# Softmax denominators of a four-stage attention and mixing kernel: the last 64 keys added on VectorE, two head pairs per group of ones-products

## The chip, the cores and the metric

The kernel runs on one core of one Trainium2 chip. The metric is the device time of one execution in microseconds (us), as the median of several runs.

## The reference, cut to what matters

Inputs are `q`, `k`, `v` of shape (4 batches, 12 heads, 448 positions, 64), a number `cap`, and the weights of two mixing blocks.

```python
scores = scale * q @ k.T                       # per head, 448 x 448
scores = cap * tanh(scores / cap)
attn = exp(scores - max(scores))
attn = attn / (sum(attn) + 1e-9)               # the denominators
x = attn @ v                                   # heads side by side: (4, 448, 768)

theta = x @ w_theta                            # first block, d_model 768
y = w_tok_r @ (x * cos(theta)) + w_tok_i @ (x * sin(theta))
u = x + y
x = u + relu(u @ w_ch)

h = (relu(x.T @ w_tok1) @ w_tok2).T            # second block
u = x + h
out = u + relu(u @ w_ch1) @ w_ch2              # 768 -> 1536 -> 768
```

All of it is computed in float32 accuracy. Attention multiplies in plain float32 (scores of batches 2 and 3 as three products of split numbers); the mixing blocks split each factor into a high and a low part and sum three products.

## The kernel before

**Attention.** The 12 heads of a batch are worked on as 6 pairs, and `(b, hp)` names a pair (24 in all). Scores are kept transposed: keys on the partitions, the 448 queries along the free axis. A pair has its 448 keys in three chunks of 128 (c = 1, 2, 3) and a tail of 64 (c = 0). A chunk holds both heads, `[128, 2, 448]`. The tails of an even pair and of the odd pair after it share one tile `tm`: one half of the partitions for either head, the halves swapped for the odd pair. `scores` (line 1027) does a chunk's products, then tanh and exp on ScalarE over 128x896; `av` (line 1062) multiplies exp(scores) by `v` into a PSUM tile; `LAG` chunks lie between the two.

**Denominators.** `sums` (line 1077) runs after each chunk of `av`. VectorE adds chunks 2 and 3 to chunk 1 in place (`SUMS`). At the pair's last chunk TensorE multiplies by ones: two products over the tail (with `mine`, which picks a head's half of the partitions) and two over the summed chunks, each into 32 rows of one PSUM tile, with the four side by side in the array. The tail's share and the chunks' share thus land in different rows and are added later. There is one such group per pair. For batches 2 and 3 the sums share a two-bank PSUM tile (`pa`, which the scores use too) with the pair's output; for 0 and 1 both are single banks of `pm` (`ACCM`).

**Closing a pair.** The output must be multiplied by 1/denominator, spread over the 64 rows of each head. There are two ways. `close` (line 1097, batch 0, all six pairs) stays on the engines: VectorE copies the output out of PSUM and the sums with eps/2 added; TensorE regroups the sums with four small products by `sel`; VectorE takes reciprocals and spreads them along a diagonal; TensorE multiplies by `spread`; VectorE scales the output. `finish` (line 1122, the other 18 pairs) copies output and sums out on VectorE, sends the sums by DMA into a compact tile `pk`, adds and inverts them, writes them to DRAM (`sr`) and reads them back spread over 64 rows each (`dn`, two DMAs). For batches 0 and 1 the result is then split: the high part on VectorE, the low part `XHL[..., 1]` on GpSimd. For 2 and 3 it is stored to DRAM.

**What sets the order.** All instructions are recorded first and ordered by a planner (`Plan`, line 333): a simulated schedule with a cost per instruction, a priority for each one (its place in the recording plus a shift from the packed table `RANKS`), and a limited number of buffers per tag (`SB`, `PS`). The order that comes out is written to each engine's in-order queue. The recording starts with `FIRST` steps of attention; `token(0, (0,))`, the first half of the first block for batch 0, is then woven with `SECOND` more, and what is left of the attention with batch 1 and the layers behind. Each weight piece is once fetched, split into a high and a low part and cached (`convert`, line 776); `CV` says which engine does each of its four steps (scale, low, high, rest) in each phase. `EVC` gives the engine for copies out of PSUM in `sums` and `close`, for batches 0 and 1 and for 2 and 3. `TS` and `TS0` are the buffer tags that hold the exp tiles in turn.

Of the kernel before, what the change touches and what calls it, by code (L numbers as in the profile page):

```python
# [20 lines left out]
ALU = mybir.AluOpType  # L21
# [3 lines left out]
P = 128  # L25
# [15 lines left out]
EVC = 'vv'  # L41
LAG = 3
GRP = (1, 1, 1, 1)
TS = ("t", "t", "t", "ex", "ex")
TS0 = TS
AHEAD = 2
SB = {'kq': 2, 'vt': 2, 'hl': 1, 't': 3, 'tm': 2, 'sv': 2, 'dn': 1, 'xr': 2, 'pk': 3, 'rq': 2, 'w': 4, 'raw': 3, 'cw': 5, 'wg': 4, 'zx': 5, 'rc': 4, 'ex': 2}
PS = {'pa': 2, 'pm': 4, 'ph': 4}
LATEPS = ('pm', 'ph')
SUMS = ('vv','vv')  # L50
CV = ('vaav','aaav','aaav')
# [28 lines left out]
CLOSE = 1  # L80
# [4 lines left out]
ACCM = 2  # L85
QREC = 'v'
NATIVE = 2
SVA = 0
# [3 lines left out]
FIRST = 30  # L92
SECOND = 24
# [5 lines left out]
c-mE)1$Y%#(D&zt1PuiO#R*V6#odY&mjcC#yE_z$2MDeW?(Pl&in|tf4Z(s03rUa!a(CX};oSG__whW-y?1xdoSFapN6y*J@-YLn)Xfjtv0sdy>-  # L99
140b9~bEUq0%Z+c8=$=A+&`8l$B*#AsUIkGf-ej3(+DrT*JubXj<e22_gC8be}q{N`v~(I#5&1V-  # L100
!qRUb91e~f1C_)*_H|EN`Ke%9?5Vsz@BPa5+vT5DJStY4eO>A8bnG<(|^Efe}hU4dWq=M7)=qEEDbIq*UM{VQ58-t&<()xPSR8ecWTyJ+3x#Om!6U-
cK~t4<Nsl>_4RaP2P|FvhLDt~h$IkD~*x@IBZ^&Y%6NpQ^@c*U65KAL3|XKUM#WZr$42(Lt9T-
P_R7oiT3p{p8lL#Xb^z)UD0(xV8T_AIWmq(M;JL^_>%;r)#-&;6@)=)E61CZq1)wHT_h#R^HEeA4fY3b#&BtN6SugwC{2s>7P_})=IZ#TIwUiBHUWFs-rW
0bu`^aw??&abnqW;T@~oodc_>QvCh%*{;I<U`iS2FM=z9cwA2_M88XDJY5Mv|)SWo}mQM9;LmxTb%SR%^-Fo_@TNh_QN9N1c$kEC1-
cmWzt)UAXT|LLq9eGuIquaGAjy`p%K78S5NMhAFtyNRcaP*Hdsw-y3>D-%c^}g#Z{~-
U#0=FLa_mQP{94($!wP6<3%R3w$Rz>win4?h(9lh_ZI?3he+C)BbIL@tA{!r~2>n$CgxV21IM{nj*z4g-
3d2JlsUO_c7jq1xxs?9IBwQ=&KGVYeQOm3)JA3sIz_Lf1F-1_Obw}h^DbU{<qiT`?w>xiS{z#-
zGxBS4I5f2@8cDvP|u_J1z9?Rh9q_K|XjdAq!b#Ez_$w#KagGL=4^={$TI|UuhRT~|PsOJ9Q*1KuEMK*d%o<^!Ed{zBUdds)DsufG6kY6%8dbqgi)}4+X`
p3~d<sCi3TvsMI+B$IpS-HYn4%Sr71aHpq{rSOoUGlrP_<&E66sl*JdrP%B-jeWd)n26>UAD+u!Vam1u5~o*nwJDNSM9LH(X{w|^WFp!-
dVL0K5@YPM2Mp&x4L!A=Xkw*E?!q4GcaMCR#=r>!bf;Z44C@uQ+?gRTap!of4AYVx1&YiZ17Asaq8%mS&ps<ax`wcw*+?gmK;|d9gZHuyLijP`)+MASEPu  # L110
aqj};T{RzJRRUd47Ia>NJ)q=$xeNq6NdV5RzCXR0T;^^@n-g3Mfa(jA9$Wm-vLOj*;mYU_=`XRBSr&f5$y=;zlEa|8}7+r6V4?j7YK1I9^bnfZOORDEvc}
x9rK63w*qq813S`i=TL{4h_b)**h1~X4qNB>OVEe8fWdar?_x9WOJ)s(8a-n+H#JM23I7q`208yNd0Qf=oWvM65l@JH2-
i@c;A_to#H+WMiFWcG7wzJp$}<A_`56>)S^YcCns!b=M7b@Z1u@mja3mn56!)?B^ZdfVkCA;`a8NwwA<N1I-CYq4F9-
X7%EhztC#tXiR#YKZ`1CCbt6W59d<1<g}9UWfR4$v+d_dal2tUHf`TmJF&*q1Gw%>W6;S6NqTE>fZMX=~dT9D7JaY3+{VWO|^D$FR7J{_}iumeYJ>7zW*B
?t2*E<`Y>!1GA4gjjV^}H`1XmHqf6sl(x(qO<d{oJw<F(GSM9siC3DDW?TF)QeO*FG>g~O%M&7R(y(BEDqrDS4+O6|5Z8TPO<_4EsIik8PsYuvo)htn}G0
fEvU00_N`T9(?96JB}#wC8lqWhYoKL@#F$UtzotoreqYJ!heeix74&MV^hDf%EYVw+3GlvVZWs#<2WODb%D+Xq~-2cve*Q+=P`CE>$F+Wf0}pLui-
`Q@r=*i$RB_Xd8SP;Iqb^~xJnZd1~vKHACse7_c_8g$RzI}iO2bMFLnE_p?@2l;H{EHHGeUX?>tueTLRi~O0_?3hs(RR6#?kL@i|5t+DHw<dK-
B4RZBA$BwtX&0l~{*)ba;*07!=Ed!@4_$&dm*$gdLdKQ42aab%ZYE41UG|A|-z(DdACW$LMEdO(`E!>@u9M`{52`sMRjcn1Ir-ko4cjhq1id?L;s?B$3Vx
Z$8B_4zO6FRP{^!qO1HYdigi4&NiLV}G|GUwui{4=u7#-kzTaH%Te<8WZ6z*xp?~GSPZh2WdOTfLovzdP;^IlY)3f^yasdmRd=fI-
{K3sD{)d#x@aJ?d!9%ZZ#$I0`mUB;jrI3#xCn?RA4aC#nmKkLC!mZ*~YwE19>gv&$%mx%nn3VaufoOw=-  # L120
WNaQ}y&(^s^zdi(29Z7R@25?wozXcQ{ttswsHKNrtENo|FB4kvgt$(8L`)JBA2w6FnY%k<`g2T4Br*~F3gDyN$?g5`h^?pS`Ynk_A<lhbo{Qg*kDS@)k&k
PFe<#DMiW|YRugD8*7I0aMtrIv7jusizPox9(M%5D;ItW>}$^Y>8ZK$=O2lmbzMZELfWq3)942Ey_uM_jc*?f3+WEI>Grv|=Ig=P}M{6$y8`3b5Gx`-
@KDUy@%y*lw9I=#g<x7*79?mM;LNkMuR8H32jQbr^}Y5Y@4BymZR<R##FIeY()#Km&*NZ;Q?vS8B!#&@hEvJxMU28VLbt-O}`M20_5-
# [36 lines left out]
|PXsfa5u1JbgF4$`<%<8o2Z1jc0H<SpjkoJiVQte2o0=a4jUS-  # L160
EYW@jO(m}BZ%wU;6I2pu8Z8X7mQDU+f4ix$oE9}ARkzlCdr+`?uz7=<y(-?{9EB|dOj1N!&hv-LSI)3T{9E&3ujYTP-iIl;5PAH9h<9p{Pi23^*J2;Rbel
As~bH(bLHwH@)Q0m-
P^4h@!4N}RPWuk`(Lx+NhW;P7@vgEkMw6f?Dx0bmzjnQ|ExkE@Vx~eQ)0729rVX9Ly4UN_^2B`EXo?Q#BcN)#B8ZLw%0Rtt}MM`1=gD7!Dtz|t0I2AX4cK
bc>wqqC?`?~taERN2gF;qS&SvF#<P~0#P|ZtodNt8Q1h-Fh9l&nwk96HzbpM-WpM38uIWy_t$@sq^dM!?e*}Ii#`pYiX9E3uXL8^~a&lJm{~5bF@R<vKeA
~|Y@wwf%*~yr*TpRCMhqR>@7G<1SubVxGrR2>%#7cE|(vrMTjPvcdw+y}51^oP{>CdQ*A;j6Ay+t|=XMURhf%wSHJhka@?!wtN<f@P4-E-
# [448 lines left out]
def attn_mix_kernel(ctx: ExitStack, tc: tile.TileContext, kqd, vd, cap, wu, wtok, wt1, wt2, out):  # L614
# [94 lines left out]
    consts = const("consts", [5])  # L709
    capt, qscale, eps, halfpi, eps2 = (consts[:, i:i + 1] for i in range(5))  # L710
    sel = const("sel", [32])
    spread = const("spread", [P])
# [1078 lines left out]
```

## Time and profile before

| | us |
|---|---|
| median of 3 runs (lowest to highest) | 883.93 (883.5 to 884.7) |
| profiled execution | 883.66 |
| its span | 881.9 |
| TensorE (PE) busy | 869.8 (99%) |
| VectorE (DVE) busy | 727.6 (83%) |
| ScalarE (ACT) busy | 539.3 (61%) |
| GpSimd (POOL) busy | 190.2 (22%) |

The profiled execution took 1.8 us more than its span. A busy TensorE is one with a matmul in flight: matmuls overlap, so what a group of them costs is the distance from its first start to the next group's first start, not the sum of durations. A plain float32 matmul stands in the trace as two records. TensorE's clock was granted in full in every slice of the span. Nearly all instructions go through one recording helper and so carry one line number; groups are told apart by their tiles. Batch 0's attention lies in about the first 76 us, all attention in the first 368 us.

### The profile page before, as it was taken

Reading aid. Unit: us, or ns where it says so; the run is one execution under the profiler, and the core shown is the slowest. Engines: PE = TensorE matmul, PEld = TensorE weight load, DVE = VectorE, ACT = ScalarE, POOL = GpSimd, SP = SyncE. Lnnn points to the kernel's source line nnn. Section 1 sums busy time; section 2 is a strip of 40 time slices with the busy share of each in tenths; the row PEclk is TensorE's granted clock in tenths of the full one; section 3 lists DMA queues with packets and bytes.
Section 4 is the critical chain, followed back from the end, with each engine's and each line's share of the span. In section 5 each row is a group of like instructions: output and inputs, shape, how many; then the busy total and the mean of one; then the engine's idle time right before and its main releaser. Section 6 shows DMA issues by size and latency. Waiting matters only on the chain. (4 is left out here: it accounts for less than half of the span.)

```text
span 881.9 us, 13457 instructions
## 1 busy us (share of the span) xinstructions
PE 869.8 (99%) x4683; PEld 684.8 (78%) x4683; DVE 727.6 (83%) x1363; ACT 539.3 (61%) x929; POOL 190.2 (22%) x163
## 2 busy tenths in 40 slices
PE   9989999999999999999999999999999999999998
PEld 2224665657677667699999899899999999999997
DVE  6999889997875665799898899889968778958597
ACT  7998999789974565456475563755533445334251
POOL 2434232330121110012333343132210130000000
PEclk9999999999999999999999999999999999999999
DMA  6888775684478342146888898812124112745623
GB/s 194 298 307 292 224 262 182 215 275 140 147 206 311 123 140 77 48 130 221 286 298 258 312 331 297 313 37 73 42 83 151 36 54 85 227 132 190 203 88 122
DMA packets 85320, 163.35 MB, mean 185 GB/s; under 512 B 11268, under 2 KB 65156, under 8 KB 85252
## 3 DMA queue, kind: packets, MB, share of 16 engines
q1 hardware_dynamic: 85252, 162.49, 55.9%
q8 instruction: 37, 0.61, 0.3%
q14 instruction: 31, 0.25, 0.1%
HBM read 114.75 MB, written 47.58 MB: 184 GB/s over the span
## 5 line engine op out<-in xcount | busy, mean ns | idle before, releaser
L598 POOL TENSOR_TENSOR cw<-cw,raw 128x384 uint32<-128x384 uint32 (+2 forms) x94 | 106.0, 1133 | 295.4 <-DVE cw L598 117.4
L598 PE MATMUL tm<-WT,zn 128*128 128x448 f32 x504 | 112.1, 371 | 0.0
L598 PEld LDWEIGHTS tm<-WT,zn 128*128 128x128 f32 x504 | 92.4, 188 | 16.0 <-issue 6.6
L598 PE MATMUL P<-XHL,w 128*128 128x448 f32 x414 | 91.9, 364 | 0.0
L598 PE MATMUL c<-g,w 128*128 128x448 f32 x432 | 88.3, 364 | 0.0
L598 PEld LDWEIGHTS c<-g,w 128*128 128x128 f32 x432 | 81.0, 187 | 6.4
L598 ACT ACTIVATE t<-sp,consts 128x896 f32<-128x896 f32 x72 | 71.9, 1013 | 18.9 <-PE sp L598 17.4
L598 PEld LDWEIGHTS P<-XHL,w 128*128 128x128 f32 x414 | 77.5, 188 | 6.0
L598 ACT ACTIVATE t<-t,consts 128x896 f32<-128x896 f32 x72 | 75.0, 1053 | 0.7
L598 PE MATMUL P<-T,S 128*128 128x448 f32 x306 | 68.5, 365 | 0.9 <-ACT u L598 0.9
L598 ACT CAST w<-cw 128x384 fp32r<-128x384 f32 x72 | 36.5, 517 | 51.1 <-POOL cw L598 18.3
L598 PE MATMUL av<-t,vt 128*64 128x448 f32 x288 | 64.6, 556 | 1.6 <-DVE sv L598 0.7
L598 POOL TENSOR_TENSOR XHL<-XT,XHL 128x448 fp32r<-128x448 f32 x30 | 40.0, 1333 | 119.5 <-ACT XHL L598 95.0
L598 PEld LDWEIGHTS P<-T,S 128*128 128x128 f32 x306 | 57.2, 188 | 5.7 <-ACT u L598 1.3
L598 DVE TENSOR_TENSOR t<-t,t 128x896 f32<-128x896 f32 x48 | 53.4, 1112 | 3.9 <-PE av L598 2.9
L598 DVE SCALAR_TENSOR_TENSOR cw<-raw,cw 128x384 uint32<-128x384 uint32 (+2 forms) x94 | 52.5, 565 | 1.0
L598 ACT ACTIVATE raw<-raw 128x384 uint32<-128x384 uint32 (+2 forms) x94 | 48.5, 527 | 4.6 <-DMA raw<-wu 4.5
L598 PE MATMUL sp<-kq 64*128 64x448 f32 (+1 forms) x240 | 46.9, 573 | 3.6 <-ACT t L598 3.6
L598 ACT CAST S<-F 128x256 fp32r<-128x256 f32 (+1 forms) x57 | 24.5, 445 | 41.7 <-DVE F L598 38.0
L598 PE MATMUL th<-XHL,w 128*128 128x448 f32 x216 | 49.2, 372 | 0.0
L598 DVE TENSOR_TENSOR w<-cw,w 128x384 fp32r<-128x384 f32 x72 | 42.9, 601 | 7.5 <-ACT w L598 7.5
L598 PE MATMUL P<-g,S 128*128 128x448 f32 x216 | 48.6, 368 | 0.0
(163 smaller groups left out, 1797.1 us busy)
## 6 DMA issues: line engine op xcount, KB each, us to landing
w<-cu SPq DMA_DIRECT2D x40, 768.0 KB
raw<-wu SPq DMA_DIRECT2D x72, 384.0 KB
cu<-w SPq DMA_DIRECT2D x52, 384.0 KB
kq<-kqd SPq DMA_DIRECT2D x24, 448.0 KB
cu<-w SPq DMA_DIRECT2D x10, 768.0 KB
w<-cu SPq DMA_DIRECT2D x27, 256.0 KB
cs<-S SPq DMA_DIRECT2D x30, 192.0 KB
S<-cs SPq DMA_DIRECT2D x30, 192.0 KB
```

Of the source, the lines that this page charges most:

```text
L598: getattr(eng[o.eng], name)(*map(real, a), **{x: real(y) for x, y in k.items()})
```

## The change

VectorE adds the tail's two halves to chunk 1 as well (two adds of 64 partitions x 448 per pair), so one tile per pair holds all that is to be summed. `finish` is called once per two pairs, and its group of four products by ones (two heads of two pairs, 32 rows each) serves both. Only one double pair, `(0, 4)` (the last of batch 0), closes by products, with one `sel` step and two products by `spread`; the others go by DMA, one `pk` and one `sr` transfer per two pairs. Output and sums of batches 0 and 1 are copied out of PSUM by ScalarE (`EVC`), their low part is made by VectorE (`XLO`), and the output tile is always a single bank of `pm`. For weight pieces the low step of the first 11 goes from ScalarE to VectorE; from the 12th on, the scale step goes from VectorE to ScalarE. `FIRST` grows by 3 and `SECOND` falls by 3, the tags of the exp tiles change, `rq` has one buffer instead of two, and `RANKS` is another table (left out here).

```diff
-EVC = 'vv'
+EVC = 'av'
-TS = ("t", "t", "t", "ex", "ex")
-TS0 = TS
+TS = ('ex','t','t','t','t','t')
+TS0 = ('ex','zx','zx','zx','t','zx')
-CV = ('vaav','aaav','aaav')
+CVN = 11
+CLOSE = ((0, 4),)
+TAIL = 'vv'
+XLO = 'v'
+CV = ('vvav','aaav','aaav')
-FIRST = 30
-SECOND = 24
+FIRST = 33
+SECOND = 21
...
-        scale, low, high, rest_ = CV[phase[0]]
+        scale, low, high, rest_ = CV[phase[0] or int(len(done) >= CVN)]
...
         def accs(b, hp):
-            if b < ACCM:
-                acc = [psum("av"), None]
-            else:
-                acc2 = psum2("av")
-                acc = [acc2[:, 0], acc2[:, 1]]
-            st[b, hp][3] = acc
+            st[b, hp][3] = [psum("av"), None]
...
         def sums(b, hp, c, acc, pt):
+            odd = hp % 2
+            if c >= 2:
+                (pool if SUMS[b // 2][c - 2] == "p" else dve).tensor_tensor(out=pt[1], in0=pt[1], in1=pt[c], op=ALU.add)
+            if c == odd:
+                for j in range(2):
+                    r = rows(j ^ odd)
+                    (pool if TAIL[b // 2] == "p" else dve).tensor_tensor(out=pt[1][r, j], in0=pt[1][r, j], in1=pt[0][r], op=ALU.add)
+            if c == (NM if odd else 0):
+                x = XT[:, b, hp, :] if b < 2 else sbuf("xr", "xr", [S])
+                (act.copy if EV[b // 2] == "a" else dve.tensor_copy)(x, acc[0][:, :S])
+                st[b, hp][3] = x
+                if odd:
+                    finish(b, hp - 1)
+
+        def close(b, hp, sm):
             sv = sbuf("sv", "sv", [S])
+            dve.tensor_scalar(out=sv, in0=sm[:, :S], scalar1=eps, scalar2=None, op0=ALU.add)
             rq = sbuf("rq", "rq", [CP])
             with plan.fuse():
                 for q in range(NK):
+                    mm(sm[32 * q:32 * q + 32, :CP], sel, sv[:, q * CP:(q + 1) * CP], True, True, f32=True, half=0.25)
+            dve.reciprocal(out=rq, in_=sm[:, :CP])
...
+            for n in range(2):
+                dn = sm if n else psum("dn")
+                mm(dn[:, :S], spread[:, n], sv, True, True, f32=True)
+                scaled(b, hp + n, st[b, hp + n][3], dn[:, :S])
+
+        def finish(b, hp):
+            sm = psum("sm")
+            with plan.fuse():
+                for n in range(2):
+                    for j in range(2):
+                        g = 64 * n + 32 * j
+                        mm(sm[g:g + 32, :S], ones, st[b, hp + n][4][1][:, j, :], True, True, f32=True, half=0.25)
+            if (b, hp) in CLOSE:
+                return close(b, hp, sm)
+            sv = sbuf("sv", "sv", [S])
+            (act.copy if EV[b // 2] == "a" else dve.tensor_copy)(sv, sm[:, :S])
+            pk = sbuf("pk", "pk", [2, 16])[:4 * S // 16, 0]
+            sr = dram(f"sr{b}_{hp}", 4, [S], whole=True)
+            with pri(-50):
+                sp_.dma_start(pk, sv[::32].then(lambda a: a.rearrange("q (p f) -> q p f", f=16)))
+            dve.tensor_scalar(out=pk, in0=pk, scalar1=eps[:4 * S // 16], scalar2=None, op0=ALU.add)
+            dve.reciprocal(out=pk, in_=pk)
...
+            for n in range(2):
+                x = st[b, hp + n][3]
+                dn = sbuf("dn", "dn", [S])
+                with pri(-50):
+                    for j in range(2):
+                        sp_.dma_start(dn[64 * j:64 * j + 64], sr[2 * n + j:2 * n + j + 1].then(lambda a: a.broadcast_to([64, S])))
+                scaled(b, hp + n, x, dn)
+
+        def scaled(b, hp, x, dn):
+            dve.tensor_tensor(out=x, in0=x, in1=dn, op=ALU.mult)
             if b >= 2:
                 stash[b, hp] = dram(f"xd{b}_{hp}", P, [S])
                 sp_.dma_start(stash[b, hp], x)
             else:
                 dve.tensor_copy(out=XHL[:, b, hp, 0], in_=x)
-                lo_pool(XHL[:, b, hp, 1], x, XHL[:, b, hp, 0])
+                (lo_pool if XLO == "p" else lo)(XHL[:, b, hp, 1], x, XHL[:, b, hp, 0])
             del st[b, hp]
```

## Rows read from the trace of the kernel before

**Rows 1.** The page, part 1: busy time, share, instructions of TensorE.

```profile
PE 869.8 (99%) x4683; PEld 684.8 (78%) x4683; DVE 727.6 (83%) x1363; ACT 539.3 (61%) x929; POOL 190.2 (22%) x163
```

**Rows 2.** Windows of 20 us: busy time (instructions) per engine, granted clock, DMA share, GB/s.

```profile
20.00:40.00 20.00, 18.91 (x102) 5.32 (x103) 19.12 (x33) 20.00 (x29) 9.62 (x7) 1.00 0.92 312
40.00:60.00 20.00, 18.70 (x120) 5.09 (x116) 20.00 (x38) 20.00 (x29) 7.62 (x7) 1.00 0.79 270
60.00:80.00 20.00, 18.32 (x101) 7.59 (x98) 18.28 (x38) 17.02 (x24) 9.13 (x8) 1.00 0.88 305
...
100.00:120.00 20.00, 20.00 (x111) 11.72 (x111) 18.43 (x37) 19.92 (x35) 7.23 (x7) 1.00 0.82 254
...
280.00:300.00 20.00, 20.00 (x132) 15.35 (x131) 11.02 (x19) 9.11 (x13) 3.70 (x3) 1.00 0.48 163
```

**Rows 3.** Timeline of TensorE, 158 to 176 us: start, duration, engine, operation, count.

```profile
159.86 0.57 PE L598 MATMUL sm<-tm,mine 128*32 128x448 f32 x2
...
160.75 0.98 PE L598 MATMUL tp<-ident,rc 128*128 128x128 f32 x7
```

**Rows 4.** Timeline of TensorE, 60 to 80 us, with idle before in brackets.

```profile
61.14 1.02 PE L598 MATMUL sm<-sv,spread 128*128 128x448 f32 x2
62.09 1.02 PE L598 MATMUL sp<-kq 64*128 64x448 f32 x4
64.43 1.02 PE L598 MATMUL sp<-kq 64*128 64x448 f32 x4 [1.33 <-ACT t L598]
...
68.68 0.40 PE L598 MATMUL sm<-sv,sel 128*32 128x112 f32 x8
69.01 1.77 PE L598 MATMUL sp<-kq 64*128 64x448 f32 x8
...
76.50 3.70 PE L598 MATMUL th<-XHL,w 128*128 128x448 f32 x17
```

**Rows 5.** Groups by line and shape: operation, shapes, count; busy us, mean ns; idle before.

```profile
L598 PE MATMUL sm<-t,ones 128*32 128x448 f32 x48 | 11.3, 551 | 0.0
...
L598 PE MATMUL av<-t,ones 128*32 128x448 f32 x48 | 11.2, 550 | 0.0
```

**Rows 6.** The same view: VectorE and ScalarE operations that go, move or stand nearest.

```profile
L598 ACT ACTIVATE raw<-raw 128x384 uint32<-128x384 uint32 x72 | 39.6, 560 | 4.6 <-DMA raw<-wu 4.5
...
L598 ACT COPY u<-P 128x448 f32<-128x448 f32 x34 | 18.0, 529 | 29.7 <-PE P L598 29.0 <-DVE u L598 0.7
...
L598 DVE TENSOR_TENSOR XHL<-XT,XHL 128x448 fp32r<-128x448 f32 x24 | 16.3, 692 | 2.5 <-ACT XHL L598 2.5
...
L598 DVE TENSOR_TENSOR hl<-kq,hl 128x448 fp32r<-128x448 f32 x12 | 14.9, 1244 | 0.2
...
L598 DVE COPY XT<-av 128x448 f32<-128x448 f32 x12 | 7.4, 617 | 0.5 <-PE av L598 0.5
...
L598 DVE TENSOR_SCALAR cw<-raw 128x384 f32<-128x384 f32 x12 | 5.5, 466 | 3.9 <-DMA raw<-wu 3.9
...
L598 DVE RECIPROCAL rq<-sm 128x112 f32<-128x112 f32 x6 | 5.0, 847 | 0.4 <-PE sm L598 0.2
...
L598 DVE TENSOR_SCALAR sv<-sm,consts 128x448 f32<-128x448 f32 x6 | 4.1, 680 | 0.6 <-PE sm L598 0.5
...
L598 DVE TENSOR_TENSOR sv<-rq,diag 128x448 f32<-128x448 f32 x6 | 3.7, 620 | 0.0
...
L598 ACT ACTIVATE cw<-raw 128x224 f32<-128x224 f32 x8 | 3.2, 406 | 1.2 <-DVE ch L598 1.2
```

**Rows 7.** The tile `dn`: shortest/median/longest ns, first and last start, us.

```profile
L598 DVE TENSOR_TENSOR XT<-XT,dn x6: 611/615/619, 102.3 to 185.1; 128x448 f32<-128x448 f32 x6
```

**Rows 8.** The tile `pk`, same columns.

```profile
L598 SPq DMA_DIRECT2D pk<-sv x36: 502/562/867, 78.4 to 369.6; - x36
```

**Rows 9.** Timeline of VectorE, 60 to 80 us.

```profile
67.02 0.61 DVE L598 COPY XT<-av 128x448 f32<-128x448 f32 x1
67.55 1.35 DVE L598 TENSOR_TENSOR t<-t,t 128x896 f32<-128x896 f32 x1
```

More of the change, by code (lines that the diff above doesn't have):

```diff
@@ L104 @@
[L104 to L109, printed above, removed]
@@ L256 @@
+hvL|~9!v_F{|AA61L2ATJ{>oEAY?er^BvRwn(rd1nH!k95niP?`<DaMFKjBq^*ZQ39bZ4EzdAn+ec*Zk1>pYyR_A<6
 """
@@ L708, in attn_mix_kernel @@
     ident = plan.buf(lambda: ident_ap, "con", [P])
-    consts = const("consts", [5])
-    capt, qscale, eps, halfpi, eps2 = (consts[:, i:i + 1] for i in range(5))
+    consts = const("consts", [4])
+    capt, qscale, eps, halfpi = (consts[:, i:i + 1] for i in range(4))
     sel = const("sel", [32])
-    spread = const("spread", [P])
+    spread = const("spread", [2, P])
     diag = const("diag", [NK])
-    pick = const("pick", [2])
+    pick = const("pick", [4])
     ones = const("ones", [32])
-    mine = const("mine", [2, 32])
     kq0 = sbuf("kq", "kq", [2, S])
@@ L721, in attn_mix_kernel @@
     dve.memset(ones, 1.0)
-    dve.memset(mine, 0.0)
-    for j in range(2):
-        dve.memset(mine[64 * j:64 * j + 64, j], 1.0)
     with pri(30):
@@ L727, in attn_mix_kernel @@
         dve.memset(diag, 0.0)
-        for j in range(2):
-            for g in range(2):
-                dve.memset(sel[64 * g + 32 * j:64 * g + 32 * j + 1, 16 * j:16 * j + 16], 1.0)
+        for g in range(4):
+            dve.memset(sel[32 * g:32 * g + 1, 8 * g:8 * g + 8], 1.0)
         for q in range(NK):
             dve.memset(diag[32 * q:32 * q + 32, q:q + 1], 1.0)
-        for j in range(2):
-            at = pick[:, j:j + 1]
-            cols = [ident[:, 32 * q + 16 * j:32 * q + 16 * j + 1] for q in range(NK)]
+        for g in range(4):
+            at = pick[:, g:g + 1]
+            cols = [ident[:, 32 * q + 8 * g:32 * q + 8 * g + 1] for q in range(NK)]
             dve.tensor_tensor(out=at, in0=cols[0], in1=cols[1], op=ALU.add)
@@ L738, in attn_mix_kernel @@
                 dve.tensor_tensor(out=at, in0=at, in1=cols[q], op=ALU.add)
-            dve.tensor_copy(out=spread[:, 64 * j:64 * j + 64], in_=at.then(lambda a: a.broadcast_to([P, 64])))
+            dve.tensor_copy(out=spread[:, g // 2, 64 * (g % 2):64 * (g % 2) + 64], in_=at.then(lambda a: a.broadcast_to([P, 64])))
     dve.memset(halfpi, HALFPI)
@@ L745, in attn_mix_kernel @@
     dve.tensor_scalar(out=eps, in0=eps, scalar1=1e-9, scalar2=None, op0=ALU.mult)
-    dve.tensor_scalar(out=eps2, in0=eps, scalar1=0.5, scalar2=None, op0=ALU.mult)
     wt = sbuf("warm", "zx", [S])
@@ L1077, in sums @@
         def sums(b, hp, c, acc, pt):
-            mode = SUMS[b // 2]
-            end = NM if hp % 2 else 0
-            if c >= 2 and mode[c - 2] != "n":
-                (pool if mode[c - 2] == "p" else dve).tensor_tensor(out=pt[1], in0=pt[1], in1=pt[c], op=ALU.add)
-            own = [0, 1] + [i for i in (2, 3) if mode[i - 2] == "n"]
-            todo = range(len(own)) if c == end else ()
-            if todo and acc[1] is None:
-                acc[1] = psum("sm")
-            with plan.fuse():
-                for i in todo:
-                    src = pt[own[i]]
-                    for j in range(2):
-                        g = 64 * (i % 2) + 32 * j
-                        js = slice(64 * j, 64 * j + 64)
-                        a1, a2 = (mine[:, j ^ (hp % 2)], src) if own[i] == 0 else (ones, src[:, j, :])
-                        plan.rec("PE", "matmul", (acc[1][g:g + 32, :S], a1, a2), {"start": i < 2, "stop": i >= len(own) - 2}, {"f32": True, "half": 0.5 if i == 2 else 0.25})
-            if c == end:
-                finish(b, hp, acc)
-        def close(b, hp, acc):
-            x = XT[:, b, hp, :] if b < 2 else sbuf("xr", "xr", [S])
-            (act.copy if EV[b // 2] == "a" else dve.tensor_copy)(x, acc[0][:, :S])
+            odd = hp % 2
[12 more added lines that the diff above has]
+        def close(b, hp, sm):
             sv = sbuf("sv", "sv", [S])
-            if SVA:
-                act.activation(sv, acc[1][:, :S], AF.Identity, bias=eps2)
-            else:
-                dve.tensor_scalar(out=sv, in0=acc[1][:, :S], scalar1=eps2, scalar2=None, op0=ALU.add)
+            dve.tensor_scalar(out=sv, in0=sm[:, :S], scalar1=eps, scalar2=None, op0=ALU.add)
             rq = sbuf("rq", "rq", [CP])
@@ L1107, in close @@
                 for q in range(NK):
-                    mm(acc[1][32 * q:32 * q + 32, :CP], sel[:, :32], sv[:, q * CP:(q + 1) * CP], True, True, f32=True, half=0.25)
-            dve.reciprocal(out=rq, in_=acc[1][:, :CP])
-            (pool if QREC == "p" else dve).tensor_tensor(out=sv.rearrange("p (q s) -> p q s", q=NK), in0=rq.then(lambda a: a.unsqueeze(1).broadcast_to([P, NK, CP])), in1=diag.then(lambda a: a.unsqueeze(2).broadcast_to([P, NK, CP])), op=ALU.mult)
-            mm(acc[1][:, :S], spread, sv, True, True, f32=True)
```

347 lines of the change are left out of this document (160 added, 187 removed).

## The prediction

> **What bounds the kernel now.** I read the page's first part, then busy time per 20 us, then TensorE's timeline, the groups by shape, and the tiles of the closing chain. The first part shows TensorE with a matmul in flight for 869.8 of 881.9 us [rows 1]: whatever else happens, the end comes after TensorE's work plus its idle time, and the idle time is small. The windows show where it is not alone. From 20 to 60 us ScalarE is busy 20.00 of 20 us in both windows and VectorE 19.12 and 20.00, while TensorE has 18.9 and 18.7; from 60 to 80 ScalarE has 17.0 and TensorE 18.3 [rows 2]. In this stretch only attention can run, since the first product of the mixing block (`th`) starts at 76.50 [rows 4]. TensorE waits there for ScalarE's exponentials, 1.33 us in one place [rows 4]. Behind it TensorE has 20.00 of 20, with ScalarE still at 19.9 (100 to 120 us) and later at 9.1 (280 to 300 us) [rows 2]. So there are three stretches: batch 0, with three engines near full; batch 1, with TensorE full and ScalarE close behind; and the rest, where TensorE alone sets the end and the others have room. The granted clock is 1.00, the 2.4 GHz level, in each of these windows [rows 2].
>
> **The products that go.** A denominator group costs the distance from its start to the next start, 160.75 - 159.86 = 0.89 us [rows 3]. The ones-products over summed chunks have 48 + 48 records [rows 5], four per pair (two products, two records each): 24 groups. After the change there are 12, of the same four products over the same 448 columns, so 12 x 0.89 = 10.7 us go. Closing by products costs TensorE 69.01 - 68.68 = 0.33 us for `sel` and 62.09 - 61.14 = 0.95 us for `spread` [rows 4]. Six closes are 6 x 1.28 = 7.7 us; the one that stays has one `sel` and two `spread` steps, 0.33 + 1.90 = 2.2 us. So 5.5 us go, and 16.2 us in all. By stretch: batch 0 loses three groups and the closes, 2.7 + 5.5 = 8.2 us; batch 1 three groups, 2.7 us; batches 2 and 3 six groups, 5.3 us.
>
> **What VectorE gets.** 48 adds of 64 x 448. No row shows one on 64 partitions. The nearest is the multiplication of two SBUF tiles of 128 x 448, 0.615 us [rows 7]. If half the partitions halved it, it would be 0.31; the dearest row of two SBUF inputs of that width is 1.244 us [rows 6]. I take 0.615, because the work per partition is the same. The low part of 12 pairs comes over from GpSimd at 0.692 each [rows 6].
> Batch 0: 12 adds +7.4; low part 6 x 0.692 = +4.2; output copies to ScalarE 6 x 0.617 = -3.7; five closing chains fewer 5 x (0.680 + 0.847 + 0.620) = -10.7; the low step of 11 weight pieces, like the scale step on VectorE at 0.466, +5.1; the scale step of pieces 12 to 22 (30 recording steps at five pieces in seven are 22), at most 11 x 0.466 = -5.1, but 224 wide, so I take -3 [rows 6]. Sum: about -0.7 us.
> Batch 1: +7.4 + 4.2, less copies of six outputs and six sums, 12 x 0.617 = 7.4: +4.2 us. Batches 2 and 3: 24 x 0.615 - 6 x 0.617 = +11.1 us, in a stretch in which VectorE is busy for only 11 of 20 us [rows 2]; that one is hidden. If the adds cost 1.244, batches 0 and 1 get 24 x 0.63 = 15 us more, which the first 80 us cannot hide.
>
> The trace lets neighbours on VectorE overlap: a copy that starts at 67.02 and takes 0.61 is followed by a start at 67.55, 0.08 before its end [rows 9]. The Trainium skill (VectorE: DVE Perf Modes, section "Two Vector instructions with no wait between them") holds an instruction until all earlier ones have finished when it starts in another group of 32 partitions than the last one; one of each pair's two adds starts at partition 64. By that rule this add and the one behind it lose 0.08 each, 1.0 us in batch 0, and the sum would come to 873 instead of 872; no row here starts at partition 64, so nothing shows it.
>
> **What ScalarE gets.** Copies out of PSUM at 0.529 [rows 6]: 12 outputs and five sums (two double pairs of batch 0 and three of batch 1), +9.0 us. The low step of 11 pieces leaves it, 11 x 0.560 = -6.2; the scale step of 11 pieces, mostly 224 wide, comes, 11 x 0.406 = +4.5 [rows 6]. That is +7.3 us before the end of batch 1; in batch 0 alone 8 copies, +4.2 - 6.2, and as much of the 4.5 as the planner puts there: between -2.0 and +2.5.
>
> **What is moved or made to wait.** Four of batch 0's pairs now close by DMA. The first such round trip of before ran from 78.4 (sums sent) to 102.3 (output scaled), 24 us [rows 7, 8]. The early pairs have that time before `th`; the last two close by products. So I cost it at nothing; a late one would hold the first `th` back and VectorE's in-order queue with it, by up to 24 us less what is left of the stage. Transfers per two pairs fall from 10 to 6, so SP's queue gets shorter. An even pair's output and summed chunks are held until the odd pair is done, 17 us longer (two batches' 12 pairs take about 200 us). With two `xr` buffers the next output copy may wait, and a PSUM bank with it; TensorE has other products to do then, and I take 0, with 2 us as the upper end. The output of batches 2 and 3 now takes a bank of `pm`, and scores get both tiles of `pa`; batch 1 already ran so, at 20.00 of 20 [rows 2]: 0. GpSimd loses the low parts; it is busy 9.6 of 20 us there at most [rows 2] and bounds nothing.
>
> **The sum.** Behind batch 0, 8.0 us of TensorE's time go and nothing is late in its place: other products are ready. In batch 0's stretch 8.2 us go, but ScalarE and VectorE do not get less work (-2.0 to +2.5, and -0.7). What can come back there is ScalarE's idle time in the last window, 20 - 17.0 = 3.0 us, which stands behind the last closing chain, and what the planner gains by putting weight pieces and batch-1 chunks off until later, where ScalarE has 11 us free in 20 [rows 2]. I take half of the 8.2, 4 us. So 883.7 - 8.0 - 4 = 872 for the profiled execution of 883.66; the median of the runs is 883.93, 0.3 above it, and I leave that in the rounding.
>
> **Rivals.**
> *All of it comes back* (chance 0.22): the planner pushes attention of batch 1 forward or weight pieces back, so that TensorE's gaps in the first 76 us do not grow. For it: the 3.0 us that ScalarE is idle, and fewer stations in the closing chain. Against it: 40 us with ScalarE at 20.00 of 20. Time 883.7 - 16.2 = 867.5.
> *ScalarE sets the pace to the end of batch 1* (0.18): the products saved in batches 0 and 1, 10.9 us, become gaps. For it: +7.3 us on an engine that stands at 19.9 of 20 at 100 us. Against it: TensorE has the first block of batch 0 to work on meanwhile. Left are the six groups of batches 2 and 3: 883.7 - 5.3 = 878.4.
> *ScalarE gets longer than what is saved* (0.07): the same place, but its 7.3 us are all on the path, as batch 1's outputs come later and the first block of batch 0 is used up. It decides from where ScalarE's work to the end of batch 1 exceeds the stretch's length, that is when its idle time there is under 7.3 us. 883.7 - 5.3 + 7.3 = 885.7, slower than before.
> *The change doesn't do what it says* (0.06): the whole order is drawn anew with another priority table, and adds for chunk and tail queue in front of the last group, so that TensorE meets as much new idle time as the groups cost. Time within 0.2% of 883.7.
> The forecast itself has 0.47, with 867.5 to 877 as its own range (all or hardly any of batch 0's share, and adds up to 1.244).
>
> **Chances.** About 0.2%, 1.8 us, is what a measurement of this kernel tells from no change. Faster: 0.47 + 0.22 + 0.18 = 0.87. Same: 0.06. Slower: 0.07. The range takes in the first two rivals on the fast side, with 2 us below the first for waits that the new order may drop, and the 878.4 with 1.6 us for dearer adds: 865.5 to 880.
>
> **What would show it.** Ones-products: 12 groups at 0.89 apart, `sel` once and `spread` twice. 48 adds on 64 partitions near 0.6 us. TensorE's records fewer by 12 x 8 + 5 x 8 + 4 x 2 = 144, and its busy time down by 10 to 16 us. The first `th` at 68 to 77 us; if it is at 68 or earlier with gaps no larger, the first rival holds. In the windows from 20 to 60 us ScalarE stays at 20 and TensorE falls to 16 or 17 (my 4 us lost). If ScalarE is at 20 of 20 up to 160 us and TensorE under 19 there, the second or third rival holds. The prediction is wrong if TensorE shows idle time behind 80 us that was not there, by waits for VectorE's adds, for `xr` or for a PSUM bank.

## The result and the profile after

The changed kernel takes 873.85 us as the median of 4 runs (872.66 to 873.96), the kernel before 883.83 in the same session (883.5 to 884.7). The ratio is 0.9882, 95% interval 0.9865 to 0.99: 10 us, or 1.2%, faster. 872.0 was forecast, with 865.5 to 880 as the range. The profiled execution took 873.95 us, with a span of 871.9.

Part 1 of the page after, busy time, share and instructions, answers to [rows 1]:

```profile
PE 853.9 (98%) x4539; PEld 683.3 (78%) x4539; DVE 741.3 (85%) x1374; ACT 539.0 (62%) x942; POOL 178.2 (20%) x151
```

TensorE has 4683 - 4539 = 144 records fewer and is busy for 15.9 us less. Its idle time, span less busy time, went from 881.9 - 869.8 = 12.1 us to 871.9 - 853.9 = 18.0. So 5.9 of the 15.9 us came back as idle time. The windows of 20 us (busy time and instructions per engine, granted clock, DMA share, GB/s) show where, beside [rows 2]:

```profile
20.00:40.00 20.00, 18.02 (x96) 5.10 (x94) 18.20 (x35) 18.96 (x26) 6.26 (x5) 1.00 0.79 261
40.00:60.00 20.00, 16.37 (x80) 4.66 (x80) 18.41 (x30) 19.23 (x29) 4.93 (x4) 0.83 0.86 280
60.00:80.00 20.00, 17.88 (x88) 5.12 (x92) 17.38 (x34) 15.68 (x27) 3.36 (x4) 0.91 0.86 306
...
100.00:120.00 20.00, 19.57 (x104) 12.15 (x103) 18.46 (x38) 19.93 (x39) 4.13 (x4) 1.00 0.66 207
...
280.00:300.00 20.00, 20.00 (x127) 14.38 (x128) 12.02 (x21) 10.08 (x16) 1.76 (x2) 1.00 0.66 251
```

Nearly all of it lies in batch 0's stretch: up to the first `th`, TensorE's idle time went from 6.0 to 11.5 us (76.50 us with 70.52 busy, 83.57 with 72.04). From there to the first product of the next stage (`c`) it is 1.2 us in both kernels. The rest is 0.8 us less behind that and 1.1 us more behind the last product. From 40 to 80 us there is something that the kernel before did not show: granted clocks of 0.83 and 0.91. TensorE's timeline after (start, duration, engine, operation, count, idle before in brackets) has the places:

```profile
27.01 1.50 PE L597 MATMUL sm<-t,ones 128*32 128x448 f32 x8
28.44 2.48 PE L597 MATMUL av<-t,vt 128*64 128x448 f32 x12
...
43.88 1.58 PE L597 MATMUL sp<-kq 64*128 64x448 f32 x4 [2.54 <-ACT t L597]
46.55 3.36 PE L597 MATMUL sp<-kq 64*128 64x448 f32 x8 [1.09 <-ACT tm L597]
49.84 1.53 PE L597 MATMUL sm<-t,ones 128*32 128x448 f32 x8
51.29 2.48 PE L597 MATMUL av<-t,vt 128*64 128x448 f32 x12
...
66.82 1.02 PE L597 MATMUL sp<-kq 64*128 64x448 f32 x4 [1.82 <-ACT t L597]
67.77 1.57 PE L597 MATMUL dn<-sv,spread 128*128 128x448 f32 x2
69.27 3.57 PE L597 MATMUL av<-t,vt 128*64 128x448 f32 x12
72.77 0.98 PE L597 MATMUL av<-tm,vt 64*64 64x448 f32 x8
...
83.57 2.12 PE L597 MATMUL th<-XHL,w 128*128 128x448 f32 x9
```

Eight `sp` records, 1.77 us at full clock [rows 4], take 3.36 at 46.55: about twice as long, the 1.2 GHz level. The clock is down already in the four `sp` records at 43.88 (1.58 us instead of 1.02), behind the wait of 2.54 us; the wait of 1.09 lies inside the slow stretch. The second such place, 67.77 to 72.77, follows a wait of 1.82; the same twelve `av` records take 2.48 us at 51.29 and 3.57 at 69.27. Summed from start to start against the same groups at full clock, the two places cost 4.4 us (0.6 + 1.6 + 0.6 in the first, 0.5 + 1.1 in the second). The first `th` starts at 83.57 us instead of 76.50 [rows 4], though with 24 more records of batch 1's attention done before it. The first `c` comes at 373.00 us instead of 381.98, so nearly all of the gain is there by then.

The bill for TensorE's queue is then: 10.0 us shorter, with 5.9 us more idle time and 4.4 us at the lower clock, so its own products take 20.3 us less. 10.0 of that are the groups of ones-products and 5.4 the closes, where 10.7 and 5.5 were forecast. Most of the other 4.9 is in products that the change does not name: summed from start to start behind the first `th`, without idle time, the attention scores of split numbers take 1.4 us less, the mixing products `tm` and `t` 1.8 and 1.0. The counts there are the same. The scores stand in 26 runs instead of 34, so they are interrupted less often by other products. For `tm` and `t` most of it is in neighbours of the same kind, which stand closer (median start to start 201 ns instead of 203, and 114 instead of 120); what makes that is not shown. No run here has the old way of summing in a newly planned order, so the order's own part of the 10 us is not separated.

The new adds, from the groups by shape (count; busy us, mean ns; idle before) of the whole span:

```profile
L597 DVE TENSOR_TENSOR t<-t,tm 64x448 f32<-64x448 f32 x48 | 32.6, 680 | 3.7 <-ACT tm L597 2.5 <-PE av L597 0.2
```

### The profile page after: what moved, and what is told of

Same layout as the page of the kernel before. It is cut to its first block, busy times and chain, and to the rows that moved or that the text cites. A ratio compares the mean times of both kernels' runs of the same rounds, so it can differ in the third digit from the quotient of the medians.

```text
span 871.9 us, 13133 instructions
## 1 busy us (share of the span) xinstructions
PE 853.9 (98%) x4539; PEld 683.3 (78%) x4539; DVE 741.3 (85%) x1374; ACT 539.0 (62%) x942; POOL 178.2 (20%) x151
## 4 chain that ended last, share of the span: by engine, by line
PE 75%; ACT 11%; DVE 9%; DMA 2%; issue 1%; POOL 1%; SPq 0%; POOLq 0%; ACTq 0%
PE P L597 29%; PE tm L597 10%; PE c L597 8%; PE t L597 7%; PE wc L597 5%; ACT t L597 5%; PE av L597 4%; PE sp L597 4%; PE th L597 3%; DVE t L597 2%; PE tp L597 2%; DVE cw L597 2%; PE xp L597 1%; ACT L597 1%; DVE w L597 1%
## 5 line engine op out<-in xcount | busy, mean ns | idle before, releaser
L597 POOL TENSOR_TENSOR cw<-cw,raw 128x384 uint32<-128x384 uint32 (+2 forms) x94 | 103.6, 1107 | 331.5 <-DVE cw L597 191.1
L597 PE MATMUL tm<-WT,zn 128*128 128x448 f32 x504 | 110.2, 368 | 1.1 <-DVE zn L597 1.1
L597 DVE TENSOR_TENSOR w<-cw,w 128x384 fp32r<-128x384 f32 x72 | 46.2, 648 | 9.0 <-ACT w L597 8.6
L597 PEld LDWEIGHTS th<-XHL,w 128*128 128x128 f32 x216 | 39.3, 188 | 11.2 <-DVE rc L597 1.7
L597 PE MATMUL wc<-XHL,w 128*128 128x448 f32 x216 | 47.4, 370 | 0.0
```

The costliest lines, as they stand in the source:

```text
L597: getattr(eng[o.eng], name)(*map(real, a), **{x: real(y) for x, y in k.items()})
```

## The experiments

Every kernel here but one keeps the changed kernel's order on each engine. The planner is given the old durations and counts, and an instruction that moves to another engine is emitted at its planned place (`moved`). Each ratio is to the kernel before, from the same session; the changed kernel's is 0.9882 [0.9865, 0.99].

**Late groups tripled.** Does TensorE alone set the end behind batch 0?

```diff
+for again in range(3 if b >= 2 else 1):
     for n in range(2):
         for j in range(2):
             mm(sm[g:g + 32, :S], ones, st[b, hp + n][4][1][:, j, :], ...)
```

> Each group of ones-products of batches 2 and 3 is recorded three times (the result is the same), with the planned order unchanged. Two group starts that stand back to back are 0.8 us apart, so 12 extra groups are 9.6 us of TensorE. Theory (behind batch 0 TensorE alone sets the end): 873.9 + 9.6 = 883 us. Rival (the 10 us came from the new order, the PSUM banks or fewer transfers, and the products were hidden): at most 4 us more, 878 or less.

Measured: 881.82 us, ratio 0.9972 [0.996, 0.9983], 8.0 us over the changed kernel. TensorE's timeline shows a tripled group, where a single one in the changed kernel takes 0.89 us (356.68 to 357.57):

```profile
364.83 2.46 PE L597 MATMUL sm<-t,ones 128*32 128x448 f32 x24
367.23 0.87 PE L597 MATMUL t<-W,h 128*128 128x448 f32 x3
```

It stands for 2.40 us, 1.5 more than one group, 9.1 for six. Nearly all of it is in the time: TensorE sets the end in the stretch of batches 2 and 3, and the forecast's 5.3 us for it stand. Batch 1's 2.7 us were not tested so.

**Fillers in batch 0.** The opposite question for the first stretch.

```diff
+if b == 0 and c and not (c == NM and hp % 2):
+    for j in range(2):
+        mm(acc[0][rows(j), :224], zeros, pt[c][:, j, :224], False, False, ...)
```

> In batch 0, 15 of the steps that multiply by v get two more products with a stationary tile of zeros over 224 columns behind them (they add nothing), 15 x 0.40 = 6.0 us of TensorE; order unchanged. Theory (ScalarE and VectorE set the pace in batch 0, TensorE has 10 us of gaps there and falls to the 1.2 GHz level for some 10 us): the gaps take it up and the clock stays higher; 872 to 876 us, granted clock above 0.83 in the window from 40 to 60 us. Rival (TensorE's products count in batch 0 too, and its share of the saving was lost to something else): 873.9 + 6.0 = 880.

Measured: 874.68 us, ratio 0.9903 [0.9883, 0.9923]: 0.8 us for 6 us of products. The windows:

```profile
40.00:60.00 20.00, 16.34 (x94) 5.79 (x90) 17.29 (x30) 18.57 (x28) 5.89 (x4) 0.91 0.86 262
60.00:80.00 20.00, 17.54 (x98) 5.45 (x94) 18.29 (x33) 16.96 (x28) 3.19 (x4) 1.00 0.90 312
```

So 6 us of products before the first `th` cost next to nothing, and the 0.8 us is within the noise. The granted clock rose from 0.83 and 0.91 to 0.91 and 1.00, and the time was not shorter for it. The first of these rises need not be the fillers' work: the kernel with tripled late groups, which has the changed kernel's batch 0, shows 0.91 from 40 to 60 us without them (and 0.91 again from 60 to 80).

**ScalarE's load in batch 0.** The forecast named this engine as the one that takes the saved time back.

```diff
-act.activation(t, sp[:, :, :S], AF.Tanh, scale=qscale)
-act.activation(t, t, AF.Exp, scale=capt)
+act.activation(t, sp[:, :, :S], AF.Exp, scale=qscale)       # batch 0 alone
+act.activation(t[:, :, :8], t[:, :, :8], AF.Exp, scale=capt)
```

> In batch 0 the exponential is taken straight from the scores and the second pass covers 8 of 448 columns per head (tanh is left out); order unchanged. 21 instructions of 1.05 us become short, about 17 us less on ScalarE in the first 83 us. Theory (ScalarE sets batch 0's pace, with VectorE next to it): first theta product 5 to 9 us earlier, time 865 to 869. Rival (VectorE's queue and the closing by DMA set it): less than 2 us earlier, time above 871.5.

Measured: 873.81 us, ratio 0.9888 [0.9873, 0.9902]: nothing. The window shows that the load is gone and TensorE is no better off, and the chain of waits (start, length, what) shows why:

```profile
40.00:60.00 20.00, 15.17 (x74) 4.34 (x72) 16.05 (x29) 13.32 (x28) 6.75 (x4) 0.83 0.84 263
```

```profile
43.61 0.55 DVE cw L597
44.19 1.84 POOL cw L597
46.07 0.39 issue
46.47 1.01 ACT tm L597
47.48 0.04 issue
47.52 3.36 PE sp L597 x8
```

From 9.62 to 44.2 us every longer piece of this chain is VectorE's, but for short gaps of issue: conversion of weight pieces (`cw`, `raw`, `w`) and additions of chunks (`t`). Then GpSimd adds the piece's parts, ScalarE gets to the tail's tanh in its in-order queue, and TensorE's scores follow after 3.87 us of waiting. My theory that ScalarE's load sets the pace fell.

This is the chain with ScalarE relieved. In the changed kernel itself the long wait is another one, 2.54 us at 43.88, and it is for ScalarE's own work. ScalarE's timeline after:

```profile
40.10 2.00 ACT L597 ACTIVATE t<-t,consts 128x896 f32<-128x896 f32 x2
41.97 0.94 ACT L597 CAST w<-cw 128x384 fp32r<-128x384 f32 x2
42.78 1.04 ACT L597 ACTIVATE t<-sp,consts 128x896 f32<-128x896 f32 x1
```

Two exponentials and two casts of weight pieces stand ahead of the tanh (42.78) that TensorE waits for. Without the exponentials' length this wait falls to 0.96 us, and the next one, for the tail's tanh, grows from 1.09 to 3.87. The wait moves instead of going away.

**VectorE's tail adds cut short.**

```diff
-tensor_tensor(out=pt[1][r, j], in0=pt[1][r, j], in1=pt[0][r], op=ALU.add)
+tensor_tensor(out=pt[1][r, j, :8], in0=pt[1][r, j, :8], in1=pt[0][r, :8], op=ALU.add)
```

> The 48 tail adds run over 8 columns instead of 448, so most of the tail is left out of the denominators; order unchanged. It takes about 0.5 us each off VectorE, 6 us in batch 0 and 25 in all. Theory (VectorE and ScalarE are both full in batch 0, later adds are hidden): first theta product 0 to 4 us earlier than 83.6, time 870.5 to 873.5. Rival (the adds are what gave batch 0's share back): first theta product at 77 or earlier, time 867 or less.

Measured: 870.4 us, ratio 0.9848 [0.9833, 0.9863]: 3.5 us less. The window of 60 to 80 us stands at the full clock again, and TensorE's timeline has the twelve `av` records at 2.48 there:

```profile
60.00:80.00 20.00, 17.19 (x96) 5.13 (x92) 16.91 (x39) 16.97 (x28) 3.77 (x6) 1.00 0.89 313
```

```profile
65.80 1.02 PE L597 MATMUL sp<-kq 64*128 64x448 f32 x4 [1.82 <-ACT t L597]
66.76 1.02 PE L597 MATMUL dn<-sv,spread 128*128 128x448 f32 x2
67.71 2.48 PE L597 MATMUL av<-t,vt 128*64 128x448 f32 x12
```

Summed as above, this kernel loses 2.5 us at the lower clock instead of 4.4, so about 1.9 of the 3.5 us are the clock; whether the narrow adds brought that is open, since the changed kernel's batch 0 showed 0.83 in one execution and, with late groups tripled, 0.91 in another. The groups up to the first `th` take 0.7 us less. TensorE's idle time up to the first `th` is no shorter (12.4 us against 11.5), and the waits near 43 and 46 us are still there, 2.53 and 1.65. The time lies just below the theory's range and well above the rival's. The adds cost something, but they do not make the long waits.

**Both loads taken away.** The two edits above in one kernel.

> Both loads taken away at once: batch 0's tanh left out with its second pass over 8 columns only (some 17 us less ScalarE), and all 48 adds of the last 64 keys over 8 columns (some 6 us less VectorE in batch 0; most of the tail is missing from the denominators). Alone, the first gave nothing (873.8) and the second 3.5 us (870.4). Theory that the two engines are tied in batch 0's stretch, so that relief of one meets the other: together 863 to 868, with the first product of the mixing block at 78 us or earlier. Rival, a third thing holds the stretch (TensorE's stretch at the 1.2 GHz level, the transfers of weight pieces): 869.5 to 871.5, as the narrow adds alone.

Measured: 869.92 us, ratio 0.9842 [0.9824, 0.986], 0.5 us under the narrow adds alone, which is within the noise. ScalarE's relief gives nothing in either company, so ScalarE is not tied with the adds. What holds the place is in the chain of waits of this kernel:

```profile
40.52 1.84 POOL cw L597
...
42.80 1.01 ACT tm L597
...
43.85 3.31 PE sp L597 x8
```

Behind the conversion of a weight piece on VectorE, GpSimd adds its parts; ScalarE's cast waits 2.92 us for that, the tail's tanh stands behind the cast, and TensorE waits 3.94. By this chain the conversion of weight pieces is the third thing. No kernel here takes it away, so that is read from the trace and not tested.

**One part undone: the low step of the first 11 pieces back on ScalarE.**

```diff
 times(low, lw, lw, 2.0**-29)
+if phase[0] == 0 and len(done) < CVN:
+    plan.ops[-1].moved = "ACT"        # as act.mul
```

> One part undone: the low step of the first 11 weight pieces goes back from VectorE (0.42 us) to ScalarE (0.56 us), each at its place in the order of the changed kernel. Until about 50 us VectorE loses 4.6 us and ScalarE gets 6.2. Theory that VectorE's queue of conversions and adds sets the pace of the first 80 us (the chain of waits runs through it from 20 to 48 us): the TensorE waits near 43 and 46 us shrink, 870 to 873. Rival, both engines are equally full and ScalarE's tanh and exponentials come later: 875 to 879.

Measured: 876.07 us, ratio 0.9912 [0.9897, 0.9926]: 2.2 us more than the changed kernel, the rival (the two intervals barely overlap). ScalarE has no room for 6.2 us more (20.00 of 20 from 20 to 40 us), so this part of the change is needed, though taking load from ScalarE as it stands gives nothing.

**Two loads moved from VectorE to GpSimd.** First batch 0's tail adds, then the low parts of the outputs (which undoes that part).

```diff
 dve.tensor_tensor(out=pt[1][r, j], in0=pt[1][r, j], in1=pt[0][r], op=ALU.add)
+plan.ops[-1].moved = "POOL"           # batch 0
```

```diff
 lo(XHL[:, b, hp, 1], x, XHL[:, b, hp, 0])
+plan.ops[-1].moved = "POOL"
```

> The 12 adds of the last 64 keys in batch 0 go from VectorE (0.62 us each, 7.4 us) to GpSimd, at their places in the order. GpSimd is busy about half of that stretch and has no row of 64 x 448; from its adds of weight pieces about 1 us each is to be expected. Theory that VectorE's queue sets batch 0's stretch: a part like that of the narrow adds comes forward, 870 to 873. Rival, the longer adds stand before the weight pieces' adds on GpSimd, for which ScalarE's conversions wait: 874 to 878.

> One part undone: the 12 low parts of the attention outputs go back from VectorE (0.56 us each) to GpSimd, at their places in the order. 3.4 us of VectorE's time in batch 0 and 3.4 in batch 1. Theory that VectorE's queue sets the stretch: most of these stand from 62 us on, behind the largest waits, so at most 1 to 2 us come back, 871.5 to 873.5. Rival, that TensorE's order alone sets it from 70 us on: 873.5 to 875.

Measured: 874.33 us, ratio 0.9895 [0.988, 0.9909], and 873.6, ratio 0.9883 [0.9866, 0.9899]. Neither moves the time. The groups of the first kernel from 20 to 60 us show what the adds cost on GpSimd:

```profile
L597 POOL TENSOR_TENSOR t<-t,tm 64x448 f32<-64x448 f32 x11 | 14.1, 1284 | 9.8 <-PE av L597 6.3 <-DVE t L597 3.2
```

1.28 us each, and VectorE's own conversions get longer beside them: the last step of a piece (`w<-cw,w`) takes 1037 ns there on average, against 732 in the changed kernel.

**The low step of weight pieces on GpSimd.** First of the first 11 pieces, then of all pieces of the attention stage.

```diff
 times(low, lw, lw, 2.0**-29)
+if phase[0] == 0 and len(done) < CVN:    # second kernel: phase[0] == 0
+    plan.ops[-1].moved = "POOL"          # as pool.tensor_scalar
```

> The low step of the first 11 weight pieces goes from VectorE (0.42 us) to GpSimd, which is busy 5 to 6 of 20 us there and does the next step of the same piece anyway; all else at its place. No row shows this step on GpSimd; its add of a piece, 0.84 to 0.92 us, is the nearest. VectorE loses 4.6 us before 50 us without ScalarE getting more. Theory of the tie: 1 to 3 us come back, 870.5 to 873. Rival, GpSimd's step is on the piece's path and delays ScalarE's conversions: 874 to 877.

> As the last one, and the low step of the later pieces of the attention stage goes from ScalarE (0.30 to 0.56 us) to GpSimd too: 13 fewer steps on ScalarE, some 5 us, between 50 and 160 us, where it is busy 19.9 of 20 and TensorE lacks 1.2 us. Theory: what the first 11 give and up to 1.2 us more, 869.5 to 872.5. Rival as before: 874 to 877.

Measured: 872.89 us, ratio 0.9875 [0.986, 0.9889], and 872.1, ratio 0.9867 [0.9852, 0.9882]: 1.0 and 1.8 us under the changed kernel, and the second is the best of the kernels that leave nothing out. Both intervals overlap with the changed kernel's, so neither gain is clear of the noise. The groups from 20 to 60 us, VectorE's `cw<-cw` shift in the changed kernel and then in the first of these:

```profile
L597 DVE TENSOR_SCALAR cw<-cw 128x384 uint32<-128x384 uint32 x7 | 2.4, 341 | 0.0
...
L597 DVE TENSOR_SCALAR cw<-cw 128x384 uint32<-128x384 uint32 x7 | 4.2, 601 | 0.1
```

GpSimd's new step in the first of these:

```profile
L597 POOL TENSOR_SCALAR raw<-raw 128x384 uint32<-128x384 uint32 x7 | 10.5, 1501 | 0.6
```

I had the step at 0.84 to 0.92 us. It takes 1.50, and VectorE's shift beside it goes from 0.34 to 0.60. VectorE is busy for 19.65 and 19.37 us in the windows from 20 to 60, more than the 18.20 and 18.41 with the step on it. Up to 60 us its busy time went from 51.2 to 52.5 us, though 4.6 us of work had left it: all of the load came back, and some more.

**One part undone: a second double pair closed by products.**

```diff
-CLOSE = ((0, 4),)
+CLOSE = ((0, 2), (0, 4))
```

> One part undone for one double pair: heads pairs 2 and 3 of batch 0 close by products again (one sel and two spread steps, 2.4 us more TensorE), so the close by DMA, whose denominators were only sent at 74.18 us behind a waiting transfer and used at 82.33 and 90.25, is gone. Theory that this late close holds the first product of the mixing block: it starts 3 us or more earlier and the time is 869 to 872. Rival, that nothing waits for the late close (VectorE reaches its multiplication without idle time): the products are only added, 874 to 876.5.

Measured: 888.72 us, ratio 1.0054 [1.0039, 1.0069], 15 us more, which neither expects. This is the one kernel whose order was planned anew: other instructions for the close, the same priorities for all others. Its windows show that the loss is spread far behind the close:

```profile
100.00:120.00 20.00, 16.76 (x84) 9.98 (x82) 14.67 (x32) 19.90 (x33) 3.25 (x5) 1.00 0.71 208
120.00:140.00 20.00, 18.79 (x96) 13.27 (x93) 14.89 (x29) 19.43 (x32) 3.28 (x3) 1.00 0.57 177
```

Where it closes by products, TensorE waits 0.96 us for the sums from VectorE before `sel` and 1.95 before `spread`. But from 100 to 140 us it lacks 4.5 us where nothing was closed so, which points to the new order. What the second close alone costs stays open.

**The tail back on TensorE in batch 0, with shared groups.**

```diff
-tensor_tensor(out=pt[1][r, j], in0=pt[1][r, j], in1=pt[0][r], op=ALU.add)   # batch 0
...
 mm(sm[g:g + 32, :S], ones, st[b, hp + n][4][1][:, j, :], True, False, ...)
+mm(sm[g:g + 32, :S], ones[r], st[b, hp + n][4][0][r], False, True, ...)
```

> The last 64 keys of batch 0 go back to TensorE and the groups stay shared: the 12 adds are gone from VectorE (7.4 us), and each of batch 0's three groups gets four products over 64 keys more (from 0.89 to at most 1.8 us, 2.7 us in all). All else at its place in the order. Theory that VectorE's queue sets batch 0's stretch up to about 44 us and that products there cost next to nothing (6 us of fillers cost 0.8): 870.5 to 872.5, a version that beats both kernels, with the first product of the mixing block 1 to 3 us earlier. Rival, the products are on the path: 875 to 877. If VectorE's 7.4 us are met by ScalarE at once: 873.5 to 874.5.

Measured: 884.94 us, ratio 1.0009 [1.0, 1.0018], 11 us more. No expectation had it, since my price for the products was wrong. TensorE's timeline of one group, and the two long waits:

```profile
27.50 0.94 PE L597 MATMUL sm<-t,ones 128*32 128x448 f32 x2
28.36 0.94 PE L597 MATMUL sm<-tm,ones 64*32 64x448 f32 x2
29.23 0.94 PE L597 MATMUL sm<-t,ones 128*32 128x448 f32 x2
...
34.44 2.48 PE L597 MATMUL av<-t,vt 128*64 128x448 f32 x12
...
48.29 1.02 PE L597 MATMUL sp<-kq 64*128 64x448 f32 x4 [2.54 <-ACT t L597]
50.96 3.24 PE L597 MATMUL sp<-kq 64*128 64x448 f32 x8 [1.65 <-ACT tm L597]
```

In the changed kernel four products, each into its own 32 columns of the array, take 0.89 us together where they are not held. Here neighbours share their 32 columns in pairs, and products over 128 keys alternate with products over 64; each takes 0.87 by itself: 6.94 us a group, 16.3 more in all than the changed kernel's three groups (1.43, 1.45 and 1.65), where I had 2.7. Which of the two keeps them from running side by side, the run does not tell. VectorE's windows fell to 11.98 and 11.40 of 20, so its relief was real, and the waits of 2.54 and 1.65 us stand all the same: VectorE's load does not make them here. Of the 16.3 us, 11 are in the time, so products in batch 0 are free only as far as they fit into waits. What the tail on TensorE costs at the price that I had in mind, the kernel does not answer. The same products with all four chunks first and then all four tails were not run.

## Why the prediction was right, point by point

- **The groups and closes that go.** Right in the counts: 144 records, 12 groups, one `sel` step and two by `spread`. Not every group is 0.89 us long: eight are, batch 1's first stands for 0.96, and batch 0's three for 1.43, 1.45 and 1.65. At 27.01 and 60.80 the odd pair's products start 0.55 and 0.71 us behind the even pair's, as they wait for VectorE's adds; at 49.84 the clock is low. Groups and closes save 15.4 us at the full clock, against 16.2 in the sum. That TensorE's busy time fell by 15.9 is partly chance, as the lower clock and the new order are in it too.
- **All 8.0 us behind batch 0 come through.** Right in its reason, too small in its size. The tripled groups show TensorE setting the end for batches 2 and 3; for batch 1 it is read from the windows alone. About 4 us more came from products that the change does not name, in the new order, a term that the sum did not have and whose cause is shown only in part.
- **Half of batch 0's 8.2 us come back as gaps.** This step failed in size and in reason. All of it came back and some 2 us more: 5.5 us of idle time up to the first `th` and 4.4 at the lower clock, a term that the sum did not have. I took the loss as ScalarE's load, because it stood at 20.00 of 20 [rows 2]. It fell to 18.96 and 19.23, and taking 17 us off it changed nothing, alone or together with VectorE's adds. The two long waits near 44 and 47 us add up to 3.6 us in the changed kernel, to 4.2 with VectorE's adds narrowed or gone, and to 4.8 and 4.7 with ScalarE relieved, alone and with the adds narrowed. So no single load makes them. They are for a place in ScalarE's in-order queue, behind its own exponentials and casts or, with those short, behind a cast that waits for a weight piece from VectorE and GpSimd. The narrow adds, 3.5 us, are the only relief that showed clearly, and about half of it is the clock. Which step would have to go to win the rest back stays open.
- **The two misses cancelled.** About 4 us more gained behind batch 0, about 6 us more lost in it: 873.85 against 872.0. The number was right by a balance that I had not foreseen.
- **ScalarE to the end of batch 1** (the second and third rivals). ScalarE has 19.93 of 20 from 100 to 120 us, as forecast, and TensorE has 19.57 and lacks 1.2 us in all up to 160 us, most of it in two waits for the mixing block's `zn` (0.42 and 0.67 us). Neither rival held. The idle time behind 80 us that would have been a sign of error did not come either: from the first `th` to the first `c` it is 1.2 us before and after.
- **The tail add at 0.615 us.** Right: 0.62 for each one that stands alone in the timeline; the mean of 0.680 has stretched ones in it.
- **Adds in another group of partitions do not overlap** (the Trainium skill, VectorE: DVE Perf Modes, section "Two Vector instructions with no wait between them"). VectorE's timeline after:

```profile
34.08 0.54 DVE L597 SCALAR_TENSOR_TENSOR cw<-raw,cw 128x384 uint32<-128x384 uint32 x1
34.65 0.62 DVE L597 TENSOR_TENSOR t<-t,tm 64x448 f32<-64x448 f32 x1
35.30 1.06 DVE L597 TENSOR_SCALAR cw<-raw 128x384 f32<-128x384 f32 x1
36.40 0.62 DVE L597 TENSOR_TENSOR t<-t,tm 64x448 f32<-64x448 f32 x1
37.05 0.23 DVE L597 TENSOR_SCALAR pk<-pk,consts 112x16 f32<-112x16 f32 x1
37.20 0.61 DVE L597 TENSOR_TENSOR t<-t,tm 64x448 f32<-64x448 f32 x1
37.73 0.24 DVE L597 RECIPROCAL pk<-pk 112x16 f32<-112x16 f32 x1
```

  Around the adds at 34.65 and 36.40 each start comes 0.03 to 0.04 us behind the end ahead of it; the instruction behind the add at 37.20 starts 0.08 before its end. The rows do not name the partition at which an add starts, but that one kind of add overlaps and another does not, with about 0.1 us lost on either side, agrees with the rule and with the 1.0 us that the sum would have got for batch 0.
- **Late closes by DMA at nothing.** It held, though narrowly. For the second double pair the request for the denominators (`dn`) went out only at 74.18 us, behind a transfer of `vt` in SP's in-order queue, 11.8 us after the reciprocals had left (62.35). VectorE came to the multiplication at 82.33 without idle time, and the first `th` had no idle time ahead of it. Neither engine waited for it.
- **The first `th` at 68 to 77 us.** Wrong: 83.57, with more attention done ahead of it and more waits.

## What to carry to other kernels

When two in-order engines stand near full beside a third, busy shares do not say which of them holds it. Take the load off each engine in turn, and read the chain of waits in the kernel as it is and in the relieved one: the wait can move to another engine at the same place. Removing products from an engine that waits for others gains little in that stage, and here the wider gaps came with a lower clock as well. Price products stage by stage: 9.1 us more behind batch 0 cost 8.0, while 6 us more in batch 0 cost 0.8, and 16.3 us there, more than the waits can hold, cost 11.

## What was not expected of the hardware

- Waits of 1 to 2.5 us in a stage with TensorE busy for 16 to 18 of 20 us were followed by stretches at the 1.2 GHz level, 4.4 us lost in all. The kernel before, with one wait of 1.24 us and one of 1.33 in that stage, showed none. A wait of the same length need not bring it: with the narrow adds the wait of 1.82 us, at 65.80, was followed by products at the full clock.
- Four products over 128 keys in four groups of 32 columns take 0.89 us together where none is held; eight in which neighbours share a group of columns and alternate between 128 and 64 keys take 0.87 us each.
- GpSimd's work on weight pieces stretches VectorE's beside it: with the low step on GpSimd (1.50 us), the 128 x 384 shift on VectorE went from 0.34 to 0.60 us.
